# Finer pieces of attention, each with its own rank, engine and PSUM bank

## The chip, the cores and the metric

One core of a Trainium2 chip runs the whole kernel. The metric is the device time of one execution in microseconds (us). Five engines work side by side: TensorE (PE; its weight loads are PEld), VectorE (DVE), ScalarE (ACT), GpSimd (POOL) and SyncE (SP), which here only issues DMAs. TensorE writes its results to PSUM, which this kernel uses as eight banks of 128 x 512 fp32.

## The reference

Attention over 2 batches, 8 heads, 576 positions and 64 columns, then a gated MLP and a mixture of four experts:

```python
q_rot, k_rot = (rotate(q), rotate(k))       # x1*cos - x2*sin, x1*sin + x2*cos
scores = scale * np.matmul(q_rot, k_rot.transpose(0, 1, 3, 2))
scores = scores - np.max(scores, axis=-1, keepdims=True)
attn = np.exp(scores)
attn = attn / (np.sum(attn, axis=-1, keepdims=True) + 1e-09)
attn_out = np.matmul(attn, v)               # then (B*S, H*D) = (1152, 512)
xn = x / sqrt(mean(x*x) + 1e-6) * rms_g     # MLP, d_ff 1536
out = (silu(xn @ w_gate) * (xn @ w_val)) @ w_out
# MoE: sum over e of p_e * (relu(x @ w1[e]) @ w2[e]), four experts of width 1024
```

Everything is fp32 outside. Inside, operands of the MLP and of the experts are split into a high and a low part in TensorE's rounded fp32 format (`fp32r`).

## The kernel before, in words

Attention runs over eight *pairs*: two heads of one batch, stacked on the 128 partitions. For each pair the kernel

- loads q and k (`load_nat`, L460/465) and rotates them in four steps (`rotate`, L475, L477, L479, L488; each step has an engine),
- turns them with TensorE transposes (`turn`, L531), copies the result out of PSUM (`evac`, ACT L510, DVE L512/514) and duplicates it into a second buffer with two DMAs from SP (`dup`, L542/543),
- makes ten strips of scores (`s_step`, matmul L588; nine for the last strip's two heads share one), takes their maximum on DVE (`top`, L594) and their exponential with the sum on ACT (`exp`, L598); the strips use two pairs of PSUM banks in turn (banks 0 to 3),
- transposes the exponentials (`t_tile`, L616; the last 64 positions `t_left`, L634) and evacuates them (ACT or DVE),
- multiplies them with v in two column halves n = 0, 1 (`pv`, L656), spreads the reciprocals of the sums over the partitions with TensorE (`scale`, L696, out on ACT), and multiplies them in as DVE empties PV's bank (L668/670),
- squares the result and adds the squares up (L715, L718) for the RMS norm.

Once the four pairs of a batch are done, `rms_mean` (matmul L733, then DVE L738 to L744 and twelve tiny operations L750 to L753 for the root), `rms_spread` (L765) and `rms_apply` (DVE L777, ACT L780, the low part L781) normalize it, and the first eight tiles of the MLP (`gv_early`, matmul L797, copied out by L190) run between the later pairs. In between, weights are brought in: SP loads a block (`w_load`, L293), ACT makes a scaled copy of it into a PSUM bank (`w_first`, L323), DVE prepares the low bits (L324) and joins the two (`w_join`, L331/332), and `w_parts` splits it into high (ACT L387) and low (POOL L388). A new load waits until its buffer is given back after L388.

What sets the order: every step is an entry `[time, number, function]` in the list `program`. The entries are sorted by time, and each engine's instructions stand in the order in which the entries are called. A time is a pair's start (9 units per pair) plus an offset from a table; pairs 0, 1 and 7 have tables of their own, pairs 2 to 6 share one. A second set of tables gives engines and, by the letters x, y, z, the pair of banks that starts at 4, 6 or 7. `ps_at` (L137) takes a bank and first calls every entry that still has to use what is in it, whatever time those entries have. From about 200 us on there is only the MLP and the experts, in code that the change does not touch.

Of the kernel before, what the change touches and what calls it, by code (L numbers as in the profile page):

```python
# [10 lines left out]
I32 = mybir.dt.int32  # L11
# [10 lines left out]
    "load_k": -12.9693, "load_q": -10.4005, "load_v": -0.5176, "rot_k0": -11.2145, "rot_k1": -11.4384,  # L22
    "rot_k2": -8.9535, "rot_k3": -8.381, "rot_q0": -8.2207, "rot_q1": -7.1272, "rot_q2": -6.8011, "rot_q3": -6.1767,
    "kT": -5.757, "qT": -4.5666, "kq_evac": 0.4471, "dup": 2.4715, "S": -0.0001, "top": 0.3549, "exp": 1.2686,
    "TA": 2.1698, "TB": 2.1742, "T_out": 0.2907, "T_left": 10.7556, "left_out": 0.7573, "pv_out": 0.4247,
    "recip": 9.286, "scale": 10.9196, "scale2": 0.6376, "squares": 19.2565, "sqadd": 19.3171, "mean": 2.8979,
    "rspread": 7.5228, "apply": [9.2789, 10.1149, 10.2039, 11.2789], "apply_hi": 1.3168, "apply_lo": 3.3224,
    "w_first": [37.6368, 38.5217, 42.1088, 45.3945, 48.9843, 50.3642, 54.461, 56.7331, 75.674, 78.0411],
    "w_join": [37.7145, 39.3022, 44.7891, 47.4717, 49.5438, 51.0189, 54.865, 57.1447, 75.9344, 78.5175],
    "w_parts": [38.5649, 41.7102, 46.3127, 48.7519, 50.7782, 53.0468, 56.9871, 63.9158],  # L30
    "gv": [61.231, 62.123, 62.9168, 63.664, 71.1541, 71.579, 75.1849, 75.217, 75.4813, 75.5574, 75.7088, 76.4029, 78.0396, 78.6595, 79.5414, 81.5593],
    "gv_out": 1.8001, "apply_hi1": 1.6338, "apply_lo1": 3.8826, "mean1": 3.2922, "rspread1": 4.1145,
    "apply1": [5.3989, 5.8989, 6.4385, 6.8989], "gv_late": [2.9543, 3.8935, 3.9726, 7.2505], "turn_over": 2.4552,
    "raws1": 18.7658, "raws2": 13.7538, "pv00": 10.9055, "pv01": 11.892, "pv10": 14.8134, "pv11": 17.2589,
    "S1": 1.105, "fill": [-2.7303, -2.3443, -0.0625, 0.2994, 2.1955],
# [21 lines left out]
    "T_left": 9.6603, "scale": 9.9553, "squares": 11.1998, "sqadd": 11.4658, "recip": 9.6514, "pv_out": 0.077,  # L57
    "left_out": 4.6155, "turn_over": 0.9933, "load_q": -11.0926, "T_out": 1.5594, "qT": -5.3166, "rot_q1": -6.6561,
# [13 lines left out]
}  # L72
ENG0 = {
# [4 lines left out]
}  # L78
ENG1 = {
# [4 lines left out]
}  # L84
ENGL = {
# [4 lines left out]
}  # L90


@with_exitstack
def attention_moe_kernel(ctx, tc, q, k, v, w_gate, w_val, w_out, rms_g, probs, w1, w2, rope, out):
# [42 lines left out]
    def ps_at(i, n, later):  # L137
        for bank in range(i, i + n):
            for entry in users.get(bank, ()):
                do(entry)  # L140
        users.update((bank, later) for bank in range(i, i + n))
        return PS[:, i : i + n, :]

    def ps_big(later=()):
        nbig[0] += 1
        return ps_at(2 * (nbig[0] % 2), 2, later)
# [5 lines left out]
    program = []  # L152

    def at(time, fn, *args):
        program.append([time, len(program), fn, args])
        return program[-1]

    def do(entry):
        if len(entry) == 4:
            entry.append(True)  # L160
            entry[2](*entry[3])
# [555 lines left out]
    def add_squares(eng):  # L717
        eng.tensor_add(ssum, ssum, sq)  # L718
# [548 lines left out]
```

## Time and profile before

| | |
|---|---|
| median of 3 runs | 784.96 us (784.46 to 785.84) |
| the profiled execution | 784.8 us |
| its span, first to last instruction | 783.0 us |
| busy TensorE over the span | 754.7 us (96%) |
| busy DVE, ACT, POOL | 450.2, 347.8, 384.2 us |
| mean granted clock of TensorE, share of full | 0.989 |

All rows below come from the profiled execution, in microseconds from the start of its span. In a row `PTX<-PS 128x512` means: tile PTX is written, PS (PSUM) read, in that shape. `[0.84 <-ACT PTX L510]` means that the engine had been idle for 0.84 us and that the ACT instruction on line 510 that wrote PTX ended the wait. [...]

Stages of the attention part, by the time at which TensorE spreads a pair's reciprocals (L696): pair 3 at 81.57 us, pair 4 at 103.48 us, pair 5 at 134.48 us. The first MLP tile begins after 134 us; the second batch's norm ends before 200 us.

### The profile page before, as it was taken

The page shows a single profiled execution, that of the slowest core. Times are in us where ns is not written, and L with a number is a line of the kernel's source. Part 1 is how long each engine was busy: PE and PEld are TensorE (multiplying, and loading weights), DVE is VectorE, ACT ScalarE, POOL GpSimd, SP SyncE. Part 2 cuts the span into 40 slices and gives each one's busy share as a digit, 9 for nine tenths or more (in the row PEclk, how much of TensorE's full clock was granted, in tenths as well). Part 3 has the DMA queues.
Part 4 walks back from the last instruction along what each step waited for, and adds up shares of the span by engine and source line. Part 5 has one row for each costly group of instructions (what it writes and reads, how often), then busy time and mean ns, then how long its engine had stood idle before and what let it go on. Part 6 is the DMA issues. An engine that isn't in the chain of part 4 may idle for free.

```text
span 783.0 us, 14113 instructions
## 1 busy us (share of the span) xinstructions
PE 754.7 (96%) x5590; PEld 661.6 (85%) x5590; DVE 450.2 (57%) x807; ACT 347.8 (44%) x651; POOL 384.2 (49%) x309
## 2 busy tenths in 40 slices
PE   7999987999999999999999999999999999999997
PEld 6655554668999989999999898998989889898996
DVE  5666848455588886767584444434444544444542
ACT  3877747653546354234444243342433324143330
POOL 6445564411364476228635646455554555646440
PEclk9999978999999999999999999999999999999999
DMA  4433424220111333305102120201102020110002
GB/s 115 108 93 107 139 77 115 78 69 2 49 61 54 90 110 100 107 28 159 57 1 55 28 81 20 62 27 54 54 28 81 2 81 28 54 56 0 1 28 95
DMA packets 43473, 50.00 MB, mean 64 GB/s; under 512 B 7184, under 2 KB 35600, under 8 KB 43408
## 3 DMA queue, kind: packets, MB, share of 16 engines
q1 hardware_dynamic: 42576, 48.66, 21.0%
q8 instruction: 44, 0.72, 0.4%
q10 hardware_dynamic: 832, 0.44, 0.2%
q14 instruction: 21, 0.17, 0.1%
HBM read 43.19 MB, written 2.36 MB: 58 GB/s over the span
## 4 chain that ended last, share of the span: by engine, by line
PE 80%; DVE 8%; issue 4%; ACT 4%; POOL 3%; DMA 1%; ACTq 0%; DVEq 0%; POOLq 0%
PE PS L924 26%; PE PS L982 25%; PE PS L797 9%; PE PS L863 7%; PE PS L656 6%; PE PS L588 3%; PE PS L616 1%; ACT PP L598 1%; DVE nm L594 1%; ACT PTX L510 1%; POOL WS L401 1%; PE PS L696 1%; POOL WS L388 1%; DVE RAW L332 1%; POOL HB L968 1%
## 5 line engine op out<-in xcount | busy, mean ns | idle before, releaser
L982 PE MATMUL PS<-WL,HB 128*128 128x512 f32 x675 | 165.0, 390 | 0.0
L982 PEld LDWEIGHTS PS<-WL,HB 128*128 128x128 f32 x675 | 126.4, 188 | 27.2
L924 PE MATMUL PS<-XT,WS 128*128 128x288 f32 x960 | 140.3, 295 | 0.2 <-DVE PP L936 0.2
L956 POOL TENSOR_TENSOR HB<-PP,HB 128x1152 fp32r<-128x1152 f32 x32 | 86.0, 2686 | 101.1 <-ACT PP L955 100.6
L924 PEld LDWEIGHTS PS<-XT,WS 128*128 128x128 f32 x960 | 131.6, 188 | 0.4 <-DVE PP L936 0.4
L924 PE MATMUL PS<-XN,WS 128*128 128x288 f32 x720 | 108.8, 295 | 1.5 <-ACT PP L930 1.5
L797 PE MATMUL PS<-XN,WS 128*128 128x288 f32 (+1 forms) x672 | 104.4, 313 | 0.7 <-ACT GV L190 0.3
L797 PEld LDWEIGHTS PS<-XN,WS 128*128 128x128 f32 x672 | 101.1, 188 | 3.6 <-issue 1.3
L924 PEld LDWEIGHTS PS<-XN,WS 128*128 128x128 f32 x720 | 100.2, 188 | 2.7 <-ACT PP L930 1.9
L990 DVE SCALAR_TENSOR_TENSOR X<-PS,pr,X 128x512 f32<-128x512 f32 x63 | 46.7, 749 | 67.6 <-PE PS L982 67.6
L954 ACT ACTIVATE HB<-PP 128x1152 fp32r<-128x1152 f32 x32 | 37.3, 1167 | 106.1 <-DVE PP L938 106.1
L594 DVE TENSOR_REDUCE nm<-PS 128x1 f32<-128x576 f32 x72 | 54.0, 752 | 43.5 <-PE PS L588 36.7
L863 PE MATMUL PS<-HB,WL 128*128 128x288 f32 (+1 forms) x528 | 76.6, 305 | 0.6 <-ACT X L869 0.6
L863 PEld LDWEIGHTS PS<-HB,WL 128*128 128x128 f32 x528 | 76.1, 188 | 0.8 <-ACT X L869 0.8
L401 POOL TENSOR_TENSOR WS<-RAW,WS 128x512 fp32r<-128x512 f32 (+1 forms) x40 | 48.0, 1219 | 34.8 <-ACT WS L400 28.5
L931 DVE TENSOR_TENSOR PP<-PS,PP 128x288 f32<-128x288 f32 x40 | 18.3, 458 | 79.8 <-ACT PP L930 72.4
L598 ACT ACTIVATE PP<-PS,nm 128x576 f32<-128x576 f32 x72 | 53.3, 740 | 10.2 <-DVE nm L594 9.5
L588 PE MATMUL PS<-KQ 64*128 64x288 f32 (+1 forms) x304 | 53.3, 453 | 4.0 <-ACT PP L598 3.4
L401 POOL TENSOR_TENSOR WS<-AR,WS 128x512 fp32r<-128x512 f32 (+1 forms) x40 | 46.6, 1182 | 21.2 <-ACT WS L400 18.5
L982 PE MATMUL PS<-WS,HB 128*128 128x512 f32 x189 | 54.0, 394 | 0.0
L656 PE MATMUL PS<-PTX,VN 128*64 128x288 f32 x320 | 49.4, 446 | 0.2
L510 ACT ACTIVATE PTX<-PS 128x512 f32<-128x512 f32 (+4 forms) x70 | 38.3, 558 | 21.7 <-PE PS L616 19.2
(138 smaller groups left out, 1026.0 us busy)
## 6 DMA issues: line engine op xcount, KB each, us to landing
RAW<-in_moe_w_dram SPq DMA_DIRECT2D x16, 512.0 KB, 3.6
AR<-in_moe_w_dram SPq DMA_DIRECT2D x16, 512.0 KB, 3.6
RAW<-in_moe_w_gate_dram SPq DMA_DIRECT2D x10, 512.0 KB, 3.6
RAW<-in_moe_w_val_dram SPq DMA_DIRECT2D x6, 512.0 KB, 4.7
RAW<-in_moe_w_out_dram SPq DMA_DIRECT2D x6, 512.0 KB, 3.5
AR<-in_moe_w_out_dram SPq DMA_DIRECT2D x6, 512.0 KB, 4.4
AR<-in_moe_w_val_dram SPq DMA_DIRECT2D x6, 512.0 KB, 4.8
KQ<-KQ SPq DMA_DIRECT2D x16, 144.0 KB, 2.5
```

Source lines behind the costliest of these rows:

```text
L401: eng.tensor_sub(dst(1), src, f32(dst(0)))
L510: nc.scalar.activation(dst, src, AF.Copy, scale=1.0 if scale is None else scale)
L588: nc.tensor.matmul(box[0][rows, n, 0:HS], lhsT=queries(pair, i, c, n == i), rhs=keys(pair, i, n, n == i), start=True, stop=True,)
L594: nc.vector.tensor_reduce(nm[:, buf, j : j + 1], box[0][:, :, 0:HS], axis=AX.XY, op=ALU.max, negate=True)
L598: nc.scalar.activation(pp(pair, t)[:, o : o + S].rearrange("p (n t) -> p n t", n=2), box[0][:, :, 0:HS], AF.Exp, bias=nm[:, buf, j : j + 1 ...
L656: nc.tensor.matmul(box[0][HALF[h], :], lhsT=VN[:, pair % 2, 5 * h + k, :], rhs=PT[pair % 2][:, 4 if k == 4 else 5 * h + k, cols], start=(k ...
L797: nc.tensor.matmul(ps[:, 0:n], lhsT=w[:, lw, d, :], rhs=XN[:, lx, d, tok], start=(i == 0), stop=(i == 3 * ND - 1))
L863: nc.tensor.matmul(ps[:, 0:n], lhsT=w[:, lw, d * P : (d + 1) * P], rhs=hb(f, lx, tok), start=(i == 0), stop=(i == 11))
L924: nc.tensor.matmul(ps, lhsT=w[:, lw, a, k, :], rhs=xs(b, lx, k, c), start=(i == 0), stop=(i == 5))
L956: nc.gpsimd.tensor_sub(lo, q, f32(hi))
L982: nc.tensor.matmul(ps, lhsT=hb(f, lx, slice(t * P, (t + 1) * P)), rhs=w[:, lw, :], start=(i == 0), stop=(i == 11),)
L990: nc.vector.scalar_tensor_tensor(OA[:, t, :], in0=ps, scalar=p, in1=OA[:, t, :], op0=ALU.mult, op1=ALU.add)
```

## The change

Each entry gets a number of its own in three new tables. `PLACE` (806 ranks) replaces the time as the sort key for the entries of the attention part. `PICK` names the engine of those entries that have a choice (a, v, p for ACT, DVE, POOL), and `BANK` the first PSUM bank of those that take one. The old tables stay, with other numbers, for what the three leave open. Some entries are cut into smaller ones, so that each piece has a rank: the three copies of `t_left`, PV by each of its five strips k, the two operations of `recip`, the two copies of `scale`, the low bits of `w_first` (now `w_low`), the low part of `w_parts` (now `w_rest`), and each early MLP matmul group in halves.

```diff
+PLACE = [
+    0, 8, 1, 3, 4, 9, 2, 6, 14, 22, 29, 5, 7, 20, 10, 12, 30, 23, 13, 28, 25, 21, 40, 42, 24, 43, 52, 31, 49, 61, 38,
...
+PICK = (
+    "............v..v..............................a.a.v.a.a.v.a.a.aaa...............vap....pvvppvpp.a..a"
...
+BANK = (
+    "......444446..4..............................6.4.4.6.4.6.4.4.4...6.....7.......4...............6..6."
...
-    def ps_at(i, n, later):
+    def ps_at(i, n, later, fixed=False):
+        x = BANK[current[0]] if current[0] < len(BANK) and not fixed else "."
+        i = i if x == "." else int(x)
...
     def at(time, fn, *args):
-        program.append([time, len(program), fn, args])
+        n = len(program)
+        program.append([PLACE[n] if n < len(PLACE) else time, n, fn, args])
...
+    def pick(eng):
+        x = PICK[current[0]] if current[0] < len(PICK) else "."
+        return eng if x == "." else x if isinstance(eng, str) else {"a": nc.scalar, "v": nc.vector, "p": nc.gpsimd}[x]
...
-            eng.tensor_scalar(b.bitcast(I32), b.bitcast(U32), 2.0**-29, 7.0, op0=ALU.mult, op1=ALU.min)
             halfway.append((key, pair, raw))
+            if program:
+                lows.append((eng, b))
+            else:
+                w_low(eng, b)
...
-        eng.tensor_sub(lo, x, f32(hi))
+        rest.append((eng, lo, x, hi, key, slot, raw))
+        if not program:
+            w_rest()
+
+    def w_rest():
+        eng, lo, x, hi, key, slot, raw = rest.pop(0)
+        pick(eng).tensor_sub(lo, x, f32(hi))
...
-            evac(engs[0], pt[:, 0:5], x[:, 0])
-            evac(engs[1], pt[:, 5:9], x[:, 1, 0:4])
-            evac(engs[2], pt[HALF[1], 4], x[HALF[1], 1, 4])
+            if i == 0:
+                evac(engs[0], pt[:, 0:5], x[:, 0])
+            elif i == 1:
+                evac(engs[1], pt[:, 5:9], x[:, 1, 0:4])
+            else:
+                evac(engs[2], pt[HALF[1], 4], x[HALF[1], 1, 4])
...
         for time, ks in zip(times, ((0, 1, 2), (3, 4))):
-            later.append(at(time, mm, ks))
+            for k in ks:
+                later.append(at(time, mm, (k,)))
...
         for m in range(2):
-            later.append(at(times[m], mm, m))
-        later.append(at(times[1] + POS["gv_out"], lambda: copy(engine("gv0"), dst, box[0][:, :, 0:HS])))
+            for h in range(2):
+                later.append(at(times[m], mm, m, range(2 * h, 2 * h + 2)))
+        later.append(at(times[1] + POS["gv_out"], lambda: copy(pick(gv0), dst, box[0][:, :, 0:HS])))
```

The number of matmuls and of elementwise operations is the same. In the attention part, 12 operations of the second root (L750 to L753) go from DVE to POOL, with three of the four low parts of the second norm (L781); five rotation steps go from DVE to POOL; of the eight early MLP tiles six are copied out by DVE in place of ACT; seven copies of `t_left` and five of `scale` go from ACT to DVE; two of the low weight parts (L388) go from POOL to DVE. PV's second half of pairs 2, 3 and 5 goes from bank 7, which it shared with `w_first`, to bank 6; `w_first` itself used bank 7 ten times and now uses it six times, bank 5 three times and bank 6 once.

The order itself is best seen at three places. The line numbers after the change are those of the new file; the names are the same.

First SP at the start of the program, where it issues the loads and the duplicates of pair 0 (`64x288` is the first half of k, `64x576` is q). Before:

```order
L542 DMA KQ_75<-KQ 64x288
L543 DMA KQ_75<-KQ 64x288
L460 DMA AR<-in_q_dram 128x2x256
L465 DMA AR<-in_q_dram 64x64 x2
L542 DMA KQ_75<-KQ 64x576
L543 DMA KQ_75<-KQ 64x576
```

After (L628/629 are `dup`, L544/549 `load_nat`, L580/583 `load_v`):

```order
L544 DMA AR<-in_q_dram 128x2x256
L549 DMA AR<-in_q_dram 64x64 x2
L628 DMA KQ_75<-KQ 64x288
L629 DMA KQ_75<-KQ 64x288
L580 DMA VN<-in_v_dram 128x256
L583 DMA VN<-in_v_dram 64x64
L580 DMA VN<-in_v_dram 128x256
L583 DMA VN<-in_v_dram 64x64
L628 DMA KQ_75<-KQ 64x576
L629 DMA KQ_75<-KQ 64x576
```

Both duplicates now come after loads that they preceded, the second one after the four loads of v as well.

Second TensorE from the last strips of pair 4's first PV half (103 to 121 us in the profile), with the mean of batch 0 (L733) and both turns of pair 6 (L531). Before:

```order
L656 MATMUL PS<-PTX,VN 64x288 x4
L733 MATMUL PS<-ones,AR_77 128x1 x4
L733 MATMUL PS<-ones,AR_77 64x1
L588 MATMUL PS<-KQ_75 128x288
L588 MATMUL PS<-KQ 128x288
L616 MATMUL PS<-ident,PP 128x64 x10
L656 MATMUL PS<-PTX,VN 64x288 x10
L531 MATMUL PS<-ident,AR 128x64 x10
L588 MATMUL PS<-KQ 128x288
L588 MATMUL PS<-KQ_75 128x288
L616 MATMUL PS<-ident,PP 128x64 x8
L531 MATMUL PS<-ident,AR 128x64 x10
```

After (L746 is PV, L702 the transposes, L617 the turns, L674 the scores, L830 the mean):

```order
L617 MATMUL PS<-ident,AR 128x64 x10
L674 MATMUL PS<-KQ_75 128x288
L674 MATMUL PS<-KQ 128x288
L702 MATMUL PS<-ident,PP 128x64 x10
L746 MATMUL PS<-PTX,VN 64x288 x4
L702 MATMUL PS<-ident,PP 128x64 x8
L746 MATMUL PS<-PTX,VN 64x288 x6
L830 MATMUL PS<-ones,AR_77 128x1 x4
L830 MATMUL PS<-ones,AR_77 64x1
L674 MATMUL PS<-KQ 128x288
L674 MATMUL PS<-KQ_75 128x288
L617 MATMUL PS<-ident,AR 128x64 x10
```

The ten calls of PV's second half are two groups of four and six with transposes between them; the mean has moved behind them, and the first turn of pair 6 in front of them.

Third DVE at the same place, with the join of a weight block (L331/332) and the two products that empty PV's second half (L668, L670). Before:

```order
L668 TENSOR_TENSOR X<-PS,AR_77 128x224
L670 TENSOR_TENSOR X<-PS,AR_77 128x64
L594 TENSOR_REDUCE nm<-PS 128x1
L512 COPY KQ<-PS 128x2x5x64
L324 TENSOR_SCALAR RAW<-RAW 128x512
L331 SCALAR_TENSOR_TENSOR RAW<-PS,RAW 128x512
L332 SCALAR_TENSOR_TENSOR RAW<-PS,RAW 128x512
L594 TENSOR_REDUCE nm<-PS 128x1
```

After (L403 is `w_low`, L409/410 the join, L472 `w_rest`, L758/760 the products, L680 the maximum, L815 the sum of squares):

```order
L758 TENSOR_TENSOR X<-PS,AR_77 128x288
L815 TENSOR_TENSOR AR_77<-AR_77 128x576
L680 TENSOR_REDUCE nm<-PS 128x1
L472 TENSOR_TENSOR WS<-RAW,WS 128x512
L403 TENSOR_SCALAR RAW<-RAW 128x512
L409 SCALAR_TENSOR_TENSOR RAW<-PS,RAW 128x512
L410 SCALAR_TENSOR_TENSOR RAW<-PS,RAW 128x512
L758 TENSOR_TENSOR X<-PS,AR_77 128x224
L760 TENSOR_TENSOR X<-PS,AR_77 128x64
```

The weight block is joined ahead of the products, not behind them, and one low weight part and one sum of squares now stand on DVE here.

## Rows read from the trace of the kernel before

**Rows 1.** by stretch: start and end, length, then as the page names them; PEclk third from last.
```profile
0.00:29.35 29.35, 22.86 (x382) 17.13 (x382) 17.46 (x40) 15.13 (x33) 17.47 (x28) 1.00 0.51 127
29.35:81.57 52.22, 49.45 (x608) 31.62 (x608) 35.65 (x57) 39.59 (x95) 26.92 (x29) 1.00 0.39 104
81.57:134.48 52.91, 43.63 (x423) 27.04 (x420) 38.00 (x68) 34.28 (x79) 28.21 (x38) 0.84 0.38 106
134.48:180.03 45.55, 42.20 (x451) 29.07 (x448) 21.67 (x37) 27.21 (x63) 13.07 (x11) 1.00 0.21 63
```

**Rows 2.** what TensorE waited for, 81.57 to 134.48: us in total, times, longest.
```profile
PE PS L531 <- DVE RAW L332: 2.4, 1, 2.4
PE PS L588 <- ACT PP L598: 1.7, 4, 0.8
PE PS L616 <- DVE PTX L512: 1.0, 1, 1.0
...
PE PS L616 <- ACT PTX L510: 0.8, 1, 0.8
...
PE PS L531 <- DVE X L670: 0.7, 1, 0.7
PE PS L588 <- DMA KQ<-KQ: 0.6, 1, 0.6
```

**Rows 3.** TensorE's own lines: start, length, line, tile, count, [idle before].
```profile
89.06 1.68 PE L656 MATMUL PS<-PTX,VN 128*64 128x288 f32 x12
...
100.55 3.10 PE L656 MATMUL PS<-PTX,VN 128*64 128x288 f32 x12
...
109.82 4.34 PE L656 MATMUL PS<-PTX,VN 128*64 128x288 f32 x20
```

**Rows 4.** shorter stretches of the same view as Rows 1.
```profile
96.63:103.47 6.84, 6.30 (x40) 3.75 (x41) 4.91 (x9) 5.31 (x14) 4.43 (x4) 0.50 0.01 3
110.50:114.00 3.50, 3.50 (x18) 1.57 (x14) 0.00 (x0) 0.13 (x1) 2.85 (x10) 0.54 0.00 0
116.00:118.40 2.40, 0.12 (x4) 0.00 (x0) 1.93 (x5) 1.88 (x4) 0.00 (x0) 1.00 1.03 330
118.50:124.00 5.50, 4.27 (x55) 2.92 (x55) 5.35 (x9) 3.63 (x8) 2.74 (x3) 1.00 0.06 12
127.40:134.30 6.90, 6.14 (x38) 3.62 (x40) 6.13 (x14) 4.84 (x14) 3.39 (x4) 0.51 0.51 146
```

**Rows 5.** VectorE around the weight split, 114 to 118.
```profile
114.23 0.39 DVE L668 TENSOR_TENSOR X<-PS,AR 128x224 f32<-128x224 f32 x1 [4.66 <-PE PS L656]
114.54 0.21 DVE L670 TENSOR_TENSOR X<-PS,AR 128x64 f32<-128x64 f32 x1
...
116.90 0.69 DVE L331 SCALAR_TENSOR_TENSOR RAW<-PS,RAW 128x512 int32<-128x512 int32 x1 [0.37 <-ACT PS L323]
```

**Rows 6.** ScalarE at the scaled weight copy.
```profile
93.11 0.65 ACT L323 ACTIVATE PS<-RAW 128x512 f32<-128x512 f32 x1 [2.57 <-DVE X L668]
```

**Rows 7.** SyncE's DMA issues at the start.
```profile
13.41 0.59 SPq L543 DMA_DIRECT2D KQ<-KQ  x1
```

**Rows 8.** GpSimd, one row for each kind of operation.
```profile
89.64 1.29 POOL L388 TENSOR_TENSOR WS<-RAW,WS 128x512 fp32r<-128x512 f32 x1 [1.33 <-ACT WS L387]
...
122.51 0.82 POOL L475 TENSOR_TENSOR AR<-AR,X 128x288 f32<-128x288 f32 x1
...
127.06 1.41 POOL L479 TENSOR_TENSOR AR<-AR,X 128x576 f32<-128x576 f32 x1
...
139.31 1.56 POOL L488 TENSOR_TENSOR AR<-AR,AR 128x512 f32<-128x512 f32 x2
140.81 5.51 POOL L781 TENSOR_TENSOR XN<-X,XN 128x576 fp32r<-128x576 f32 x4
```

**Rows 9.** VectorE, the same product beside GpSimd's L388 above.
```profile
90.32 0.92 DVE L475 TENSOR_TENSOR AR<-AR,X 128x288 f32<-128x288 f32 x1
```

**Rows 10.** VectorE, the same product with GpSimd idle.
```profile
132.82 0.45 DVE L475 TENSOR_TENSOR AR<-AR,X 128x288 f32<-128x288 f32 x1
```

More of the change, by code (lines that the diff above doesn't have):

```diff
@@ L21 @@
 POS = {
[L22 to L31, printed above, removed]
@@ new lines @@
+    "kT": -5.4364, "qT": -4.1523, "kq_evac": 0.1571, "dup": 3.1572, "S": -0.0354, "top": 0.3035, "exp": 1.3749,
+    "TA": 2.152, "TB": 2.1176, "T_out": 0.5488, "T_left": 10.7627, "left_out": 1.4301, "pv_out": 0.3848,
+    "recip": 9.8233, "scale": 10.9196, "scale2": 0.7371, "squares": 19.2417, "sqadd": 21.2471, "mean": 4.1053,
+    "rspread": 8.1603, "apply": [9.4706, 10.0099, 11.0579, 13.0481], "apply_hi": 2.2909, "apply_lo": 2.8708,
+    "w_first": [37.6015, 38.5217, 42.1088, 45.3621, 48.9173, 50.3642, 54.461, 56.7331, 75.7852, 77.9536],
@@ L145, in ps_big @@
         nbig[0] += 1
-        return ps_at(2 * (nbig[0] % 2), 2, later)
+        return ps_at(2 * (nbig[0] % 2), 2, later, True)
     def ps_one():
@@ L309, in attention_moe_kernel @@
     ticks, lag, ahead, pe, JD = [0], [2], [4], [0.0], [4.0, 6.0]
-    scaled, in_psum = [], [True]
+    scaled, in_psum, lows, rest = [], [True], [], []
     lo_eng = [nc.vector]
@@ L468, in rotate @@
         x = (kn, qn)[m]
+        eng = pick(eng)
         nsin, sin, cos = (t[:, j0:j1] for t in tab)
@@ L634, in mm, with out @@
                     nc.tensor.transpose(box[0][:, r, 64 * k : 64 * k + 64], pp(pair, 4)[a, o : o + P], ident[a, a])
-        def out():
+        def out(i):
             pt = PT[pair % 2][:, :, MAIN:S]
             x = box[0][:, :, 0:320].rearrange("p r (k s) -> p r k s", s=64)
-            evac(engs[0], pt[:, 0:5], x[:, 0])
-            evac(engs[1], pt[:, 5:9], x[:, 1, 0:4])
-            evac(engs[2], pt[HALF[1], 4], x[HALF[1], 1, 4])
+            if i == 0:
[4 more added lines that the diff above has]
+                evac(engs[2], pt[HALF[1], 4], x[HALF[1], 1, 4])
         at(time, mm)
-        later.append(at(time + when("left_out"), out))
+        for i in range(3):
+            later.append(at(time + when("left_out"), out, i))
     def pv(times, pair, n, slot):
@@ L672, in pv, with recip @@
         for time, ks in zip(times, ((0, 1, 2), (3, 4))):
-            later.append(at(time, mm, ks))
+            for k in ks:
+                later.append(at(time, mm, (k,)))
         later.append(at(time + when("pv_out"), out))
-    def recip(pair):
+    def recip(pair, step):
         i = pair % 2
-        nc.scalar.activation(rr[:, i, :], sums[:, i, :], AF.Copy, bias=1e-9)
-        nc.vector.reciprocal(rr[:, i, :], rr[:, i, :])
+        if step == 0:
+            nc.scalar.activation(rr[:, i, :], sums[:, i, :], AF.Copy, bias=1e-9)
+        else:
+            nc.vector.reciprocal(rr[:, i, :], rr[:, i, :])
     def xcols(b):
@@ L699, in mm, with out @@
                     )
-        def out():
-            evac(eng, yy[:, 0:MAIN], box[0][:, 0, :])
-            evac(eng, yy[:, MAIN:S], box[0][:, 1, 0:LEFT])
+        def out(i):
+            if i == 0:
+                evac(eng, yy[:, 0:MAIN], box[0][:, 0, :])
+            else:
+                evac(eng, yy[:, MAIN:S], box[0][:, 1, 0:LEFT])
         at(time, mm)
-        later.append(at(time + when("scale2"), out))
+        for i in range(2):
+            later.append(at(time + when("scale2"), out, i))
     def squares(pair, eng):
@@ L711, in squares @@
         dst = sq if hp else ssum
+        eng = pick(eng)
         if eng is nc.scalar:
@@ L780, in rms_apply @@
         at(time + POS["apply_hi" + late], lambda: nc.scalar.activation(hi, X[:, d, both], AF.Copy))
-        at(time + POS["apply_lo" + late], lambda: eng.tensor_sub(XN[:, 1, d, both], X[:, d, both], f32(hi)))
+        at(time + POS["apply_lo" + late], lambda: pick(eng).tensor_sub(XN[:, 1, d, both], X[:, d, both], f32(hi)))
         return entry
@@ L790, in ftemp, with gv_mm @@
         return ftemps[ntemp[0] % 6]
-    def gv_mm(ps, F, ch, m):
+    def gv_mm(ps, F, ch, m, ds=range(4)):
         tok, n = ch
         w = w_get(("gv", m, F)).rearrange("p (l d f) -> p l d f", l=2, d=ND)
-        for i in range(3 * ND):
+        for i in range(3 * ds.start, 3 * ds.stop):
             d, (lw, lx) = i // 3, PASSES[i % 3]
@@ L1020, in attention_pair @@
             pv([t0 + when(f"pv{n}{i}") for i in range(2)], pair, n, slot(f"s_pv{n}"))
-        at(t0 + when("recip"), recip, pair)
+        for step in range(2):
+            at(t0 + when("recip"), recip, pair, step)
         scale(t0 + when("scale"), pair, eng["scale"], slot("s_scale"))
@@ L1082, in attention_moe_kernel @@
         at(-17, rotate, 1, nc.gpsimd, 8, 9, sq)
-        for time in POS["fill"]:
-            at(time, keep_warm, 8)
+        for i, time in enumerate(POS["fill"]):
+            at(time, keep_warm, 8, int(i < 2))
         for pair in range(PAIRS):
@@ L1101, in attention_moe_kernel @@
             at(first, w_first, engine("w_b"), [at(join, w_join)], slot("s_w"))
+            at(first, w_low)
         for i, time in enumerate(POS["w_parts"]):
             at(time, w_parts, engine("w_lo"))
+            at(time, w_rest)
         for i in range(8):
```

83 lines of the change are left out of this document (58 added, 25 removed), and 77 rows, old and new, of tables (ENG, ENG0, ENG1, ENGL).

## The prediction

> **What bounds the kernel now.** I read the table by stretches first, because the share of busy time over the whole span (96% for TensorE) mixes two kernels: from 200 us on TensorE is nearly always busy in code that the change leaves alone, so whatever happens, happens in the first 200 us. The attention stretches there differ [rows 1]. From 29 to 82 us TensorE works 49.45 of 52.22 us at the full granted clock; from 134 to 180 it works 42.20 of 45.55. Between 82 and 134 us, from the spreading of pair 3's reciprocals to that of pair 5, it works 43.63 of 52.91 us, at a mean granted clock of 0.84. That one stretch has 9.3 us of idle time, against 2.8 and 3.35 in its neighbours, and it is the only one below full clock. It is where the norm of batch 0, the weight splits and the attention of pairs 4 and 5 meet.
>
> The second view was TensorE's waits in that stretch, which say what ends each idle piece [rows 2]: the largest is 2.4 us of a turn (pair 6's q) on the join of a weight block on DVE, then exponentials on ACT and copies of transposed tiles. The third was the timeline, to see the half clock: the same PV piece of 12 matmuls takes 1.68 us at 89 us and 3.10 us at 100 us, and 20 of them take 4.34 us from 109.8 [rows 3]. [...]
>
> **The change, part by part.** All sums are against the profiled execution, 784.8 us, of which the span is 783.0; it lies 0.16 us under the median of 784.96, so that the sum needs no correction. The work is the same; what changes is which engine, which bank and what order.
>
> *82 to 134 us.* (a) Before, the turn of pair 6's q waits 2.4 us [rows 2] for the join in the bank that it takes. DVE sits idle for 4.66 us until PV's 20 matmuls are done [rows 5], and only then come the two products and, behind them, the low bits and the join. Afterwards the join stands ahead of the products and PV is in two groups. What remains late is a chain on DVE and ACT: one scaled copy 0.65 [rows 6], two join operations of 0.69, two products 0.39 + 0.21 [rows 5], and one more operation that I size like those products, 0.6: 3.2 us. Beside it TensorE has the second PV group, 12 matmuls or 1.68 us [rows 3], and the mean and scores, which I take at half of that: 2.5. A wait of about 0.8 stays: -1.6. Bounds: the whole wait goes (-2.4) or stays as long (0). (b) The scaled copy before waits 2.57 us on ACT for a product that empties PV's bank [rows 6], which is ahead of a copy that TensorE waits 0.8 us for [rows 2]; PV's half of pair 3 is in another bank now: -0.8 (0 if the copy finds another wait). (c) With the 20 PV matmuls split, DVE's 4.66 us of idle time [rows 5] can take maxima and copies. It goes in front of a stretch in which DVE is busy 5.35 of 5.50 us while TensorE loses 1.23 [rows 4]; I take half of this, -0.6, and the turn's wait for the product, -0.7 [rows 2]; bounds -1.9 and 0. (d) The half clock. The rows show no cause for it, only what came before: TensorE falls to half rate inside stretches in which it is busy about nine tenths of the time. I take half of the loss, -3.9, with bounds 0 and -7.8, since the pieces of PV are spread among other work, and nothing else in the change touches it. (e) The apply of batch 0's norm on DVE and the duplicate of pair 6, which come with waits of 0.8 and 0.6 us before [rows 2], now stand behind a weight load that waits for a low part on POOL, and that behind the root: +0.2 (-0.6 to +1.5). (f) One new wait: an exponential of pair 4 now follows the copies of the scale, a scaled copy and a plain copy on ACT. Each is of the size of the scaled copy, 0.65 [rows 6]: three are 2.0, of which 0.7, a matmul group's length, lies beside TensorE's work: +1.3. Queued behind that exponential is the next copy of transposed tiles, for which TensorE waits in its turn. (g) Three strips of scores come close together with two score buffers; the four waits of this kind before are 1.7 us in total [rows 2], so one more is about +0.5.
>
> Sum of this stretch: -1.6 - 0.8 - 1.3 - 3.9 + 0.2 + 1.3 + 0.5 = -5.6.
>
> *29 to 82 us.* All idle time is 2.77 us [rows 1]; copies go from ACT, the busier of the two (39.59 against 35.65), to DVE. I take -0.5, between -2.3 and +1.
>
> *134 to 180 us.* Idle 3.35 us [rows 1], part of it waits for copies on DVE, which gets six early-MLP copies from ACT, while the last pair's bank moves take some waits away: -0.3, between -2 and +1.5.
>
> *The start.* SP issues the second duplicate of pair 0 at 13.41 us [rows 7]. It now stands behind four loads of v; with 0.59 us for an issue as in that row this is some 2.4 us later. TensorE idles 29.35 - 22.86 = 6.5 us in this stretch [rows 1], and has other scores to make first: +0.4, between -0.5 and +1.3. Cover gone, it would cost the whole 2.4 less what the scores of the first head hide.
>
> *The second norm.* Root and three of four low parts go to POOL: four take 5.51 us there [rows 8]. The MLP pieces between them are what hides them: 0, up to +1.5. The experts: 0, the same code and order.
>
> Total: -5.6 - 0.5 - 0.3 + 0.4 = -6.0, and 784.8 - 6.0 = 778.8 us.
>
> [...] TensorE's longest gap before, 116.0 to 118.4 us, left the clock at 1.00, while it fell from 96.6 and 127.4 us on without one [rows 4]. [...]
>
> **The rivals.** *First: the clock stays whole and the waits hide.* All of (d) comes and the stretches around lose their waits at the better ends: -5.6 - 3.9 = -9.5 here, -2.3 before, -2 after: down to 784.8 - 13.8 = 771.0; I say 771 to 775.8. For it: PV's piece, which is the longest unbroken work at half clock, is cut up. Against it: the half-clock rows also hold scores and transposes [rows 4], which stay as they are.
>
> *Second: the waits change places.* The clock falls as before (0 for d), and (f) and (g) eat (b) and (c): -1.6 - 0.8 - 1.3 + 2.0 = -1.7, and with +0.4 at the start and +1 elsewhere 784.5; I say 783.5 to 786. For it: DVE is already busy 38.00 of 52.91 us there [rows 1], and almost all of the time where it is needed [rows 4]; it gets copies and low parts in addition.
>
> *Third, slower: POOL becomes the bound between the first norm's root and the early MLP.* It gets rotation steps and loses only two low weight parts. Behind the root, in the order after, stand three low weight parts (1.29 each), two pairs of rotation products (0.82 each), a square and two third steps (1.41 each), two sums of 1.56 and four low parts of the norm (5.51) [rows 8]: 3.9 + 3.3 + 4.2 + 3.1 + 5.5 = 20.0 us, of which the early MLP needs the last. TensorE's own work over the same entries I estimate at 17 us, from the 42.20 busy us of the 45.55 that follow [rows 1] and the ends of this one. At row durations POOL is thus 3 us late, which the -6.0 can absorb. But these durations are not safe: on DVE the first rotation product takes 0.92 us beside POOL's low weight part, which covers it [rows 8, 9], and 0.45 alone [rows 10]. If POOL's are stretched by 40%, it is 8 us more: 11 us late against 8.3 that the other edits leave, which is 784.8 + 2.7 = 787.5. It decides from about a quarter longer on. [...]
>
> **How the numbers follow.** The forecast (3 to 9 us faster, 775.8 to 781.8) gets 0.5; the whole clock (771 to 775.8) 0.2; waits that change places 0.16; POOL as the bound 0.14. What a measurement of this kernel can tell from no change is 0.2%, or 1.6 us: same is 783.4 to 786.5. Faster: 0.5 + 0.2 and a third of the second rival (0.06), 0.76; same: the rest of it, 0.10; slower: 0.14. The range of 8 in 10 runs from 771.5 to 786.0: it leaves out nearly all of the slower case and a little of the first rival. The likeliest case's own range is 775.8 to 781.8.
>
> **What would show it.** (a) The turn of pair 6's q with a wait on a join below 1 us. (b) The scaled copy of 93 us without a wait on PV's product. (c) DVE without an idle piece of 4 us between the scales of pairs 4 and 5, and that distance near 27 us in place of 31. (d) Granted clock above 0.9 over the stretch from pair 3's scale to pair 5's; if it stays at 0.84, the second rival is at hand. (f) A wait on ACT of about 1.3 us at pair 4's scores. At the start, the first scores at most 1.3 us later. POOL: a wait of the early MLP on a low part of the norm over 2 us speaks for the third rival. The prediction is wrong if the time from 200 us to the end changes by more than 1 us, which nothing in it allows for, or if that from pair 3's scale to pair 5's is not shorter by 3 us or more.

## The result, and the profile after

The changed kernel takes 778.18 us (777.25 to 779.69, 4 runs) where the kernel before takes 785.4 (784.46 to 786.76, 4 runs): ratio 0.9909, interval 0.9884 to 0.9933. The forecast was 778.8. The profiled execution takes 778.99 us with a span of 777.0 us, 6.0 less than before.

Where the 6.0 us come from is read from the same table by stretches, cut again where TensorE spreads the reciprocals of pairs 0, 3, 5 and 7 (columns as in [rows 1]; PEclk is the clock that TensorE was granted, as a share of full speed):

```profile
0.00:31.84 31.84, 25.42 (x383) 19.63 (x383) 19.64 (x42) 14.56 (x32) 16.18 (x28) 0.95 0.43 112
31.84:81.90 50.06, 47.56 (x600) 30.41 (x598) 34.65 (x55) 36.96 (x88) 27.54 (x30) 1.00 0.38 106
81.90:128.26 46.36, 38.55 (x411) 24.09 (x411) 35.79 (x66) 34.40 (x76) 31.42 (x42) 0.94 0.41 121
128.26:171.85 43.59, 41.89 (x456) 30.05 (x452) 27.16 (x46) 27.51 (x62) 10.79 (x9) 0.98 0.23 73
```

Pair 3's spreading comes at 81.90 us, 0.33 later than before: the start loses 2.49 us and the next stretch wins 2.16 back. From there to pair 5's it takes 46.36 in place of 52.91 us [rows 1], 6.55 less. From pair 5's to the end it is 648.74 in place of 648.52: nothing. So the whole gain lies in the one stretch in which it was forecast (-5.6), and in this pair of executions most of it is busy time, at a higher clock (43.63 to 38.55 busy, 9.28 to 7.81 idle).

These cuts don't part exactly the same work: the stretch has 411 matmuls where it had 423, ten of the twelve being the `t_left` transposes of pair 5 (0.47 us), which now come behind its spreading. Behind it the stretch up to pair 7's spreading is 1.96 us shorter (43.59 for 45.55 [rows 1]) and what follows is 2.18 longer. A cut at which the work is the same is the long piece of the MLP behind the second norm, with 3613 matmuls to the end (kernel before, then the changed one):

```profile
194.49:783.00 588.51, 582.06 (x3613) 544.22 (x3612) 330.29 (x578) 226.49 (x374) 295.73 (x202) 1.00 0.18 55
188.83:777.00 588.17, 581.91 (x3613) 544.26 (x3612) 329.66 (x577) 224.35 (x369) 299.94 (x205) 1.00 0.18 55
```

Of the 6.0 us, 5.66 are won before that point.

TensorE's waits from pair 3's spreading to pair 5's, which answer to [rows 2]:

```profile
PE PS L674 <- DMA KQ<-KQ: 3.5, 1, 3.5
PE PS L674 <- ACT PP L684: 2.2, 4, 1.0
PE PS L617 <- DVE RAW L410: 1.0, 1, 1.0
PE PS L702 <- ACT PTX L596: 0.6, 2, 0.4
```

Before, there was one more row for copies of transposed tiles than [rows 2] shows:

```profile
PE PS L634 <- ACT PTX L510: 0.9, 2, 0.5
```

The wait for the join (RAW) is 1.0 where it was 2.4, those for copies of transposed tiles (PTX) are 0.6 where they were 2.7, and one is far longer (0.6 before): 3.5 us for the duplicate of pair 6's q (KQ). It stands in SP's queue like this (start, length, line):

```profile
110.41 0.59 SPq L544 DMA_DIRECT2D AR<-in_k_dram  x1
117.99 0.37 SPq L363 DMA_DIRECT2D RAW<-in_moe_w_gate_dram  x1
118.47 0.47 SPq L628 DMA_DIRECT2D KQ<-KQ  x1
118.98 0.59 SPq L629 DMA_DIRECT2D KQ<-KQ  x1
```

SP stands at the weight load L363 for 7 us, until POOL's low weight part gives the buffer back; the duplicate is behind it. ACT has its source ready at 115.3 us. Here are TensorE's lines at the end of that wait:

```profile
120.16 0.70 PE L674 MATMUL PS<-KQ 64*128 64x288 f32 x2
124.40 0.84 PE L674 MATMUL PS<-KQ 64*128 64x288 f32 x1 [3.54 <-DMA KQ<-KQ]
```

The weight block's 512 KB move beside the duplicate (both take 6.0 us from issue to landing). And the two stretches of low clock that are left, in the stretch table of the changed kernel:

```profile
20.50:24.00 3.50, 3.50 (x34) 2.73 (x36) 2.14 (x4) 2.79 (x6) 1.75 (x3) 0.51 0.40 85
122.50:130.00 7.50, 5.60 (x42) 3.96 (x44) 3.41 (x8) 1.98 (x4) 5.54 (x6) 0.54 0.41 111
```

Those of before at 96.6 and 110.5 us [rows 4] are gone from this execution. Busy time times the missing part of the clock is 5.60 x 0.46 = 2.6 us and 3.50 x 0.49 = 1.7, in all 4.3, where before had (6.30 x 0.50) + (3.50 x 0.46) + (6.14 x 0.49) = 7.8. That sum is more than the low clock cost where the two can be compared. Run 3 below has the instructions of the kernel before up to pair 4's spreading, and in its profile the clock is 1.00 there. From pair 3's spreading to pair 4's (kernel before, then run 3):

```profile
81.57:103.48 21.91, 19.79 (x204) 12.38 (x202) 17.65 (x27) 17.06 (x40) 12.67 (x13) 0.84 0.30 84
82.65:102.86 20.21, 17.06 (x205) 10.83 (x203) 17.50 (x27) 16.13 (x38) 10.98 (x12) 1.00 0.35 91
```

The low clock from 96.6 us thus cost 1.70 us, where the sum has 3.15: at the whole clock busy time is 2.73 us less (19.79 to 17.06), but idle time is 1.03 us more (2.12 to 3.15).

Executions of one kernel also differ in how long the clock is low. Of the 45 of the kernel before that were timed beside the experiments, the ten with a mean granted clock of 0.985 take 786.7 us in the mean, the sixteen with 0.991 take 784.5 and the four with 0.993 take 783.0. The four of the changed kernel have 0.991 to 0.993 and take 777.25 to 779.69 us. At an equal clock it is 4 to 7 us faster, so that most of the gain needs no higher clock; of the 7.2 us between the medians, 1 to 2 go with it (an estimate from these means, 0.989 over the 45 and 0.992 over the four).

### The profile page after: what moved, and what is told of

Read it like the earlier page. It is cut to its first block, busy times and chain, and to the rows that moved or that the text cites. A ratio compares the mean times of both kernels' runs of the same rounds, so it can differ in the third digit from the quotient of the medians.

```text
span 777.0 us, 14117 instructions
## 1 busy us (share of the span) xinstructions
PE 751.6 (97%) x5590; PEld 661.9 (85%) x5590; DVE 454.5 (58%) x805; ACT 343.7 (44%) x635; POOL 391.9 (50%) x327
## 4 chain that ended last, share of the span: by engine, by line
PE 80%; DVE 6%; issue 5%; POOL 4%; ACT 3%; DMA 2%; SPq 1%; ACTq 0%; POOLq 0%; DVEq 0%
PE PS L1024 26%; PE PS L1082 25%; PE PS L895 9%; PE PS L963 7%; PE PS L746 5%; PE PS L674 4%; PE PS L702 2%; POOL WS L472 1%; POOL WS L485 1%; POOL HB L1068 1%; PE PS L789 1%; DMA KQ<-KQ 1%; DVE nm L680 1%; ACT PTX L596 1%; ACT PP L684 1%
## 5 line engine op out<-in xcount | busy, mean ns | idle before, releaser
L680 DVE TENSOR_REDUCE nm<-PS 128x1 f32<-128x576 f32 x72 | 53.8, 754 | 27.7 <-PE PS L674 22.2
L674 PE MATMUL PS<-KQ 64*128 64x288 f32 (+1 forms) x304 | 53.5, 453 | 9.3 <-ACT PP L684 4.6
L746 PE MATMUL PS<-PTX,VN 128*64 128x288 f32 x320 | 47.4, 420 | 0.1
L596 ACT ACTIVATE PTX<-PS 128x512 f32<-128x512 f32 (+4 forms) x63 | 36.1, 577 | 25.6 <-PE PS L702 23.6
```

Of the source, the lines that this page charges most:

```text
L596: nc.scalar.activation(dst, src, AF.Copy, scale=1.0 if scale is None else scale)
L674: nc.tensor.matmul(box[0][rows, n, 0:HS], lhsT=queries(pair, i, c, n == i), rhs=keys(pair, i, n, n == i), start=True, stop=True,)
L680: nc.vector.tensor_reduce(nm[:, buf, j : j + 1], box[0][:, :, 0:HS], axis=AX.XY, op=ALU.max, negate=True)
L746: nc.tensor.matmul(box[0][HALF[h], :], lhsT=VN[:, pair % 2, 5 * h + k, :], rhs=PT[pair % 2][:, 4 if k == 4 else 5 * h + k, cols], start=(k ...
```

## The experiments

Each changes some ranks or a bank of one of the two kernels, or one group of tables. "The changed kernel" has 778.18 us; each ratio is to the kernel before, run beside it.

**1. dup6: the duplicate ahead of the weight load.**

```diff
-PLACE[524] = 531      # turn.dup, pair 6, q
+PLACE[524] = 510.5    # w_rest, with the weight load, has 511
```

> The changed kernel with one rank altered: the duplicate of pair 6's q (two DMAs from SP) stands ahead of the weight load that waits for a low weight part on POOL, not behind it. The changed kernel's TensorE waits 3.54 us for that duplicate at 120.9 us and then works at half clock until 129.9 us. Theory 1 (the place in SP's queue, and the 512 KB weight transfer issued just ahead of it, make the wait): the duplicate is issued at about 115.3 us in place of 118.5, the wait falls below 0.5 us, and the granted clock stays whole there, which is worth 3 to 6 us: about 772 to 775 us in the end. Rival: another late thing takes its place (the norm's apply holds DVE from 119.2 to 122.7 us, and PV of pair 5 needs its bank): less than 1.5 us gained.

773.12 us (772.73 to 775.77), ratio 0.9853 (0.9828 to 0.9878). The order of the other engines stays. SP and TensorE:

```profile
114.65 0.46 SPq L628 DMA_DIRECT2D KQ<-KQ  x1
115.15 0.60 SPq L629 DMA_DIRECT2D KQ<-KQ  x1
117.34 0.37 SPq L363 DMA_DIRECT2D RAW<-in_moe_w_gate_dram  x1
```

```profile
119.49 0.70 PE L674 MATMUL PS<-KQ 64*128 64x288 f32 x4
120.45 0.53 PE L702 MATMUL PS<-ident,PP 64*128 64x64 f32 x10 [0.26 <-ACT PTX L596]
120.81 0.70 PE L674 MATMUL PS<-KQ 64*128 64x288 f32 x4
121.89 0.71 PE L746 MATMUL PS<-PTX,VN 128*64 128x288 f32 x4 [0.37 <-DVE X L875]
122.96 1.21 PE L789 MATMUL PS<-ident,rr 128*64 128x128 f32 x20 [0.36 <-DVE rr L772]
```

The wait is gone, waits of 0.3 to 0.4 us follow it, the granted clock is 1.00 from 102 to 123 us, and pair 5's spreading comes at 122.96 us, 5.3 earlier. Theory 1 holds. The low clock goes with the late duplicate in all profiles with the changed kernel's order: the six with the duplicate behind the weight load (the changed kernel, runs 4, 6 and the first two of 7) have it somewhere between 118 and 134 us, the two with it ahead (dup6, dup16) have 1.00 there. That the wait brings it isn't shown: in wfirst7 it starts at 120.6 us and in bunch2 at 118.6, ahead of waits that begin at 125.6 and 123.1. dup6 has the lowest median of the study, though that of dup16 (run 7) can't be told from it.

**2. pv3bank6: one bank, on the kernel before.**

```diff
-            pv(..., pair, n, slot(f"s_pv{n}"))
+            pv(..., pair, n, 6 if (pair, n) == (3, 1) else slot(f"s_pv{n}"))
```

> The kernel before with one thing altered: PV's second half of pair 3 is in bank 6, not in the bank of the scaled weight copy, so that the copy at 93.1 us no longer waits for the product that empties it. This is step (b) of the prediction alone, on the other kernel. Theory 1 (the waits at 92.5 to 95 us bring the low clock from 96.5 to 103.5 us, which costs 3.15 us): the ACT idle of 2.57 us goes, TensorE's wait of 0.84 goes, and the low clock there with it: 3 to 4 us faster, 781 to 782. Rival (the clock falls for what lies around it as well): 0.8 us faster and the low clock stays or comes a few us later.

782.05 us, ratio 0.9957 (0.9940 to 0.9973). The scaled copy, which waited 2.57 us in [rows 6], and the stretch that ran at 0.50 in [rows 4]:

```profile
90.65 0.63 ACT L323 ACTIVATE PS<-RAW 128x512 f32<-128x512 f32 x1
```

```profile
92.00:100.54 8.54, 7.20 (x79) 4.01 (x76) 7.31 (x13) 7.36 (x18) 4.08 (x5) 1.00 0.50 132
```

The copy waits for nothing, and the clock is 1.00 up to pair 4's spreading, which comes at 100.54 us in place of 103.48. The time is what theory 1 had, but its cause is not shown. In run 3, which has the order and the banks of the kernel before up to here, TensorE waits as it did there, and the clock stays at 1.00 from 21 to 108 us:

```profile
95.40 0.52 PE L616 MATMUL PS<-ident,PP 64*128 64x64 f32 x10 [0.85 <-ACT PTX L510]
```

In run 5, with the same instructions and the same wait again, it falls only at 100.4 us. So the wait doesn't bring the low clock of 96.5 us by itself. What the bank is worth at the whole clock is read from pair 3's spreading to pair 4's, against the 20.21 us of run 3 (first row), and the low clock comes elsewhere in this execution, as the rival had it (second row):

```profile
81.78:100.54 18.76, 17.09 (x205) 11.04 (x202) 17.44 (x27) 16.21 (x38) 10.74 (x12) 1.00 0.36 99
114.50:118.50 4.00, 3.95 (x38) 2.80 (x40) 3.70 (x7) 2.85 (x7) 1.16 (x1) 0.57 0.30 77
```

That is 1.45 us. Executions of an equal mean clock say the same: two of this kernel with 0.991 take 782.38 and 782.57 us, where the kernel before takes 784.5, and two with 0.993 take 781.33 and 781.72 against 783.0. The rest of the 3.4 us goes with a mean clock of 0.992 over these six executions against 0.989; six are too few to say whether the bank brings that too.

**3. bdup6: the duplicate ahead of the weight load, on the kernel before.**

```diff
-        at(time + when("dup"), dup)
+        at(50.7 if (pair, m) == (6, 1) else time + when("dup"), dup)
```

> The kernel before with one thing altered: the duplicate of pair 6's q ahead of the weight load on SP, as in dup6. The kernel before waits 0.57 us for it at 127.2 us, before a low clock from 127 to 134.5 us that costs 3.05 us. Theory 1: only the 0.57 us goes, since other waits (0.47 and 0.77 us on exponentials) precede the low clock, which stays: 0.3 to 0.8 us faster. Rival: the low clock goes as well: 3 to 3.6 us faster.

785.25 us, ratio 0.9998 (0.9986 to 1.0011): nothing. The 0.57 us are gone, but in the profile the clock is low from 119.5 to 137 us, and a wait of the next `t_left` is there:

```profile
119.50:137.00 17.50, 14.46 (x107) 8.95 (x107) 13.05 (x25) 11.27 (x26) 8.44 (x8) 0.51 0.38 111
```

```profile
127.92 1.33 PE L588 MATMUL PS<-KQ 64*128 64x288 f32 x4
131.62 0.79 PE L634 MATMUL PS<-ident,PP 64*128 64x64 f32 x10 [2.37 <-ACT PTX L510]
```

Neither theory had this. The same edit is worth 5 us in the new order and nothing in the old one.

**4. wfirst7: step (a) undone.**

```diff
-BANK[710] = "5"       # w_first, the block at 109.8 us
+BANK[710] = "7"
```

> The changed kernel with one bank altered: the scaled copy of the weight block at 109.8 us goes to bank 7 again, in place of bank 5, so that it waits for PV's second half of pair 4 to leave that bank, and the join stands behind PV's products on DVE. Step (a) of the prediction: the turn of pair 6's q (112.56 us, no wait) waits for the join again, 1.5 to 2.4 us, and the mean behind the join, the root and the low weight part on POOL come later with it, so that the duplicate of pair 6 does too: 1.5 to 3.5 us slower than the changed kernel. Rival: the wait of 3.54 us for the duplicate absorbs it all, since it ends there: under 0.5 us.

777.08 us, ratio 0.9893 (0.9871 to 0.9915): not slower than the changed kernel. TensorE's lines at the mean and at the end:

```profile
112.75 1.34 PE L830 MATMUL PS<-ones,AR 128*128 128x1 f32 x10 [1.96 <-ACT PTX L596]
125.80 0.76 PE L674 MATMUL PS<-KQ 64*128 64x288 f32 x4 [0.17 <-DMA KQ<-KQ]
128.01 1.21 PE L789 MATMUL PS<-ident,rr 128*64 128x128 f32 x20 [0.36 <-DVE rr L772]
```

It is not the turn that waits, but the mean, for a copy of transposed tiles on ACT. Two microseconds are lost there, the wait for the duplicate falls from 3.54 to 0.17, and pair 5's spreading comes at 128.01 against 128.26. The rival's amount holds. Its reason doesn't quite: the duplicate is issued at 119.97 us, 1.5 later than in the changed kernel, and the wait ends 1.4 later (125.80 for 124.40). That the stretch ends no later goes with the clock, which in this profile is back at 1.00 from 124 us, where the changed kernel's is low until 130.

**5. wfirst5: the bank of step (a) alone, on the kernel before.**

```diff
+   5 if first == 48.9843 else slot("s_w")
```

> The kernel before with one bank altered: the scaled weight copy at 116.2 us goes to bank 5, not 7; every engine's order stays. This is the bank's part of step (a) alone. The turn that waits 2.42 us for the join no longer shares a bank with it; the transposes behind the turn do. Theory 1: the turn and one piece of scores go ahead, and the wait, shorter by their 0.9 us and by the 0.4 us that DVE waited for the copy, moves to those transposes: 0.5 to 1.5 us faster. Rival: the copy waits for the transposes' evacuation in bank 5 and nothing is gained, within 0.5 us.

784.37 us, ratio 0.9994 (0.9975 to 1.0013). The turn waits no longer, but the eight transposes that stand ahead of it wait for the same join after the first of them:

```profile
118.72 0.46 PE L616 MATMUL PS<-ident,PP 64*128 64x64 f32 x7 [2.26 <-DVE RAW L332]
```

So nothing goes ahead: the expectation had these transposes behind the turn. No gain that can be measured.

**6. bunch and bunch2: PV's second half of pair 4 in one piece (step c).**

```diff
-PLACE[410:415] = 473, 482, 484, 486, 488
+PLACE[410:415] = 487.1, 487.2, 487.3, 487.4, 488    # bunch
+PLACE[410:415] = 473, 473.1, 473.2, 473.3, 473.4    # bunch2
```

> The changed kernel with PV's second half of pair 4 in one piece of 20 matmuls, as before the change, and not in two of 8 and 12 with transposes between. Step (c) of the prediction: DVE and ACT idle behind it again, up to 1.9 us slower than the changed kernel, and if the long piece brings the low clock (as from 110 to 114 us before, 1.7 us), up to 3.6. Rival: nothing (within 0.5 us), because the wait for pair 6's duplicate at 121 us ends at the same time whatever comes ahead of it.

786.27 us, ratio 1.0004 (0.9990 to 1.0019). In this kernel pair 6's k is duplicated before it is copied out of PSUM, so pair 6's values are others; the work is the same. PV waits 5.19 us for that copy:

```profile
114.52 5.07 PE L746 MATMUL PS<-PTX,VN 128*64 128x288 f32 x20 [5.19 <-ACT KQ L596]
```

The run says nothing on the length of the piece.

> The changed kernel with PV's second half of pair 4 in one piece of 20 matmuls again, now at the place of its first group; only TensorE's order differs, by eight transposes that come behind it. The earlier run that put the piece at the place of the last group also moved the evacuation of a turn in ACT's order, and says nothing on the length of the piece. Step (c) of the prediction: DVE idles during the piece, up to 1.9 us slower than the changed kernel, and up to 3.6 if the long piece brings the low clock. Rival: within 0.5 us of the changed kernel, because what comes later sets the end of the stretch.

779.18 us (776.25 to 780.68), ratio 0.9912 (0.9877 to 0.9946). The mean waits 0.69 us and a turn 0.76, the wait for the duplicate is 2.41 in place of 3.54. It is 1.0 us slower than the changed kernel by the medians and 0.2 by the ratios, whose interval is 2.7 us to either side: not told apart.

**7. dup0, top0, dup16: the start.**

```diff
-PLACE[16] = 30                  # dup, pair 0, q
+PLACE[16] = 22.5                # dup0: ahead of the v loads
-PLACE[25], PLACE[28] = 43, 49   # maxima of pair 0
+PLACE[25], PLACE[28] = 33.5, 33.6             # top0
-PLACE[97], PLACE[100] = 57, 72  # dup, pair 1
+PLACE[97], PLACE[100] = 54.5, 62.5            # dup16, with PLACE[524] = 510.5
```

> The changed kernel with one rank altered: the duplicate of pair 0's q is issued ahead of the four loads of v, as before the change. The changed kernel reaches the spreading of pair 0's reciprocals at 31.84 us, 2.49 us later than before. Theory 1 (the start's term of the prediction, the duplicate behind the v loads): that point comes 1 to 2.5 us earlier and the time falls by up to 2 us. Rival (the maxima on DVE, which stand behind two rotation steps that wait for POOL, and the half clock from 20.5 to 24 us, make the loss): no change at that point beyond 0.3 us.

> The changed kernel with two ranks altered: the two maxima of pair 0's second strips stand on DVE ahead of two rotation steps of pair 1, which wait for POOL for 0.7 us. Theory (DVE's queue is what delays the start): these maxima come about 0.9 us earlier (17.5 to 16.6 us), the wait of 1.07 us at 19.18 us falls to about 0.3, and if the clock then stays whole from 20.5 to 24 us another 1.7 us: the spreading of pair 0's reciprocals at 29.3 to 31.0 us in place of 31.84. Rival (the duplicate of q): nothing, since the scores then wait for that.

> The changed kernel with the duplicate of pair 6's q ahead of the weight load (as in dup6, 773.1 us) and both duplicates of pair 1 moved up in SP's queue, k's ahead of five small loads and q's ahead of a load of pair 2. In dup6 TensorE waits 1.57 us at 26.1 us for pair 1's q, issued at 25.03. Theory (that wait is the start's loss, and the place in SP's queue makes it): issued at about 23.1 to 23.9 us, the wait falls below 0.5 us and the spreading of pair 0's reciprocals comes at 29.5 to 30.0 us in place of 30.97; 1 to 1.5 us less in the end, 771.6 to 772.1. Rival: the transfer, not the issue, is late, or the next exponentials take its place: less than 0.5 us.

777.78, 777.92 and 775.19 us; ratios 0.9900 (0.9879 to 0.9922), 0.9902 (0.9880 to 0.9925) and 0.9865 (0.9847 to 0.9883). Pair 0's spreading comes at 30.87 in dup0 and 30.89 in top0, against 30.97 in dup6 and 31.02 in bunch2, whose starts are the changed kernel's own. top0's 30.89 lies where its theory had it, but the start comes as early without the edit: the 31.84 of the changed kernel's profile holds a low clock, and bunch2's start doesn't:

```profile
0.00:31.02 31.02, 23.57 (x382) 17.98 (x382) 19.13 (x42) 14.37 (x32) 16.12 (x28) 1.00 0.45 114
```

Both theories for pair 0 fail. In dup0 TensorE waits here, for pair 1's q:

```profile
25.05 0.71 PE L746 MATMUL PS<-PTX,VN 128*64 128x288 f32 x4
27.61 0.76 PE L674 MATMUL PS<-KQ 64*128 64x288 f32 x4 [1.85 <-DMA KQ<-KQ]
```

dup16 takes that wait away. Pair 0's spreading comes at 30.18, and then:

```profile
31.21 1.63 PE L746 MATMUL PS<-PTX,VN 128*64 128x288 f32 x12
34.99 0.47 PE L702 MATMUL PS<-ident,PP 64*128 64x64 f32 x8 [2.14 <-DVE AR L598]
```

The wait for DVE's copy of the scale is 2.14 us where dup6 has 0.66. Pair 1's spreading is at 50.37, in dup6 at 49.67. The gain is given back, as the rival had it, and the times of dup6 and dup16 have overlapping intervals.

**8. oldplace and oldpick: one of the tables of before in the changed kernel.**

```diff
-PLACE = [...]; POS, POS0, POS1, POSL of after
+PLACE = []; POS, POS0, POS1, POSL of before      # oldplace
-PICK = "..."; the engines in ENG to ENGL of after
+PICK = ""; the engines in ENG to ENGL of before  # oldpick
```

> The changed kernel with the order of before: no ranks, the old tables of times, but the finer pieces, the new engines and the new banks. Theory 1 (a bank that PV and the scaled weight copy no longer share is the larger part, as the run with only that bank altered showed, 3.4 us): 779 to 783 us. Rival (engines and banks were chosen for the new order, and without it they bring new waits): 784 us or more.

> The changed kernel with the engines of before: the new order and banks stay, but the rotations, copies, low weight parts and roots go back to the engines that they had. Theory 1 (order and banks carry the gain; engine moves are worth less than 1 us, as the prediction had it): 776 to 780 us. Rival (the order only works with the load taken from ACT and DVE): 782 us or more.

807.46 us, ratio 1.0293 (1.0243 to 1.0342), and 799.95, ratio 1.0177 (1.0147 to 1.0207). In oldplace the new banks pull the products of pair 2 ahead of the scales that they read, so its values differ; the work is the same. Both rivals hold, by far. In oldpick, pair 3's spreading comes 64.91 us behind pair 0's, where the changed kernel needs 50.06. One kind of wait stands out between 32 and 82 us, scores that wait for an exponential to leave their bank:

```profile
PE PS L641 <- ACT PP L651: 8.2, 5, 4.5
```

In the changed kernel these waits are 0.7 us from 31.84 to 81.90 us. The old banks with the new order and engines weren't run.

## Why the prediction was right, step by step

- **Place and sum.** -5.6 us was forecast for the stretch from pair 3's spreading to pair 5's, and it is -6.55. Ahead of it, -0.1 was forecast and +0.33 came. Behind it, -0.3 was forecast up to pair 7's spreading, with nothing after that; it is -1.96 and +2.18, since work has moved across that cut, +0.2 together. The time is within 0.6 us of the forecast. The place was foreseen for the reasons given. The amount is in part luck: (d) and (e) were both mis-sized, with opposite signs.
- **(d), the clock: right in kind, its size not shown.** "I take half of the loss, -3.9". The clock over the stretch is 0.94, as the sign asked. The loss that is halved is 7.8 us, the author's estimate from the busy time of the three stretches at 0.50, 0.54 and 0.51 [rows 4] times the missing clock. Worked out in the same way it goes to 1.9 (2.6 less the 0.7 that fall behind 128.26), which would make the term -5.9. But no run shows the 7.8 as a cost: the first of its three pieces, 3.15, cost 1.70. And executions of an equal mean clock are 4 to 7 us apart, so that 1 to 2 us go with the clock and the rest with the order and the waits. The -3.9 lies between two readings that disagree. What makes the clock fall stays open. It does not fall at one place of the program: in run 3 it falls at 119.5 us behind the 2.42 us wait for the join; in the kernel before it stays whole behind the same wait [rows 4].
- **(b), the scaled copy: more than its wait.** -0.8 was forecast. In the changed kernel the copy waits for nothing (91.88 us), and run 2 shows what the bank alone gives in the old order at the whole clock: -1.45.
- **(e), the duplicate: the term that was missed.** "+0.2 (-0.6 to +1.5)". It is the largest wait of the stretch: 3.54 us where 0.6 had been, +3.0, with a low clock from 122.5 us. The step named the queue rightly (behind a weight load, behind POOL, behind the root), but took TensorE's arrival for nearly unchanged. TensorE gets there at 120.9 us, 6.4 us earlier than in the kernel before; the issue at 118.47 is 4.6 us earlier, and the transfer takes 1.2 us longer (last section): 6.4 - 4.6 + 1.2 = 3.0. Run 1 gives all of it back, -5.1 us by the medians (-4.4 by the ratios).
- **(a), the join: measured as forecast, and worth nothing alone.** The wait is 0.95 us where 0.8 was forecast, at the other turn of pair 6. But undoing it costs nothing (run 4), and its bank alone gains nothing (run 5). In run 4 the two microseconds lost at the mean come out of the wait for the duplicate. The sum added terms that lie on one chain.
- **(c), the split of PV:** not told apart from nothing (bunch2). Its signs held: between the scales of pairs 4 and 5 DVE's longest idle piece is 3.12 us, and that distance is 25.84 us, where 27 was forecast.
- **(f) and (g), new waits for exponentials:** +1.8 forecast; they go from 1.7 to 2.2 us in all, +0.5. The waits for copies of transposed tiles, which had no term of their own but the 0.8 of (b), fall by 2.1 us.
- **The start:** +0.4, between -0.5 and +1.3. It is 2.49 in the profiled execution; in bunch2, with the same start at the whole clock, 1.67, so that the low clock from 20.5 us costs 0.8. The reason given, pair 0's duplicate behind the v loads, is refuted (dup0). TensorE waits 1.4 to 2.0 us for pair 1's duplicate in dup0, top0, dup6, wfirst7, bunch and bunch2, and taking that wait away brings pair 0's spreading 0.8 us forward (dup16). The next stretch wins the loss back.
- **Engine moves** were costed at nothing where other work hides them. The new order depends on them: without them it is 22 us slower (oldpick).
- **The rivals.** The third, POOL as the bound, does not occur: no matmul of the early MLP waits for a low part, and POOL is idle for 8 us ahead of the root. In the third's working, the 8.3 us that are set against POOL's 11 follow from no row, and POOL's low weight part covers 0.61 of the 0.92 us of [rows 9], not all. That POOL's operations would take 40% longer was the author's assumption and is not shown: its low weight parts take 1.30 us in the mean of six in the changed kernel, where one took 1.29 before [rows 8]. The second is there in part: the wait for the join has become a wait for the duplicate, and idle time in the stretch falls by only 1.47 us (9.28 to 7.81).

## What to carry to other kernels

The low clock of one profiled execution is no fixed price of the kernel. Here, with the same instructions up to there, it fell at 96.6 us in one profile and at 100.4 in another, and where these could be compared it cost 1.70 us, not the 3.15 of busy time times the missing clock. Before putting a price on it, compare executions with an equal mean clock. When several waits of one stretch are removed, ask which queue sets the end of it after that: here a DMA on SP, issued at 118.47 us behind a weight load that had stood there for 7 us until POOL was done, took back 3.0 us, more than any other single term. Order, engines and banks that were chosen together can't be costed one by one; each of the two old tables that were put back alone made the kernel slower than it had been.

## What the hardware showed beyond that

The same two DMAs of pair 6's q take very different times from issue to landing (count, KB each, median us). In the kernel before, 0.5 us behind a weight block of 512 KB:

```profile
KQ<-KQ SPq DMA_DIRECT2D x2, 144.0 KB, 4.8
```

In the changed kernel, behind such a block too:

```profile
KQ<-KQ SPq DMA_DIRECT2D x2, 144.0 KB, 6.0
```

And in dup6, which differs from the changed kernel only in that they are issued ahead of it:

```profile
KQ<-KQ SPq DMA_DIRECT2D x2, 144.0 KB, 2.4
```

Why the two behind a block differ, 4.8 and 6.0 us, no run here tells.

The place where the clock falls is not the program's alone: with the same instructions up to 110 us, it falls at 20.5 us in the profile of the changed kernel and at 11.9 in that of dup6, each time for 3 to 4 us. With those of the kernel before, up to pair 4's spreading, it falls at 96.6 us in its own profile, at 17.3 in that of bdup6, and at 11.6 and 100.4 in that of wfirst5.
